# A fourth early round of expert blocks: two blocks after batch one's rows, the experts begun two steps sooner

## The chip, the cores and the metric

The kernel runs on one core of a Trainium2 chip. A core has five engines that run side by side, each in its own fixed order: TensorE (PE, matmuls; PEld is its weight load), VectorE (DVE), ScalarE (ACT), GpSimd (POOL) and SyncE (SP, which here only issues transfers). They wait for each other through semaphores. The metric is the device time of one execution in microseconds (us). The runs of the kernel before took 1124.14, 1125.73 and 1126.33 us; the median is 1125.73.

## The reference

What is computed is a two-dimensional Fourier transform per batch, of which the real part is kept, and then a mixture of eight experts of which each row uses one:

```
x: 8 batches x 2496 rows x 256
X = fft(fft(x, axis=1), axis=2).real        -> 19968 rows of 256
logits = X @ w_gate;  e = argmax(logits)    # 8 experts
gate = softmax(logits)[e];  s = sigmoid(X @ w_output_gate)[e]
out[row] = gate * s * (relu(X[row] @ w1[e]) @ w2[e])     # w1[e] 256x1024, w2[e] 1024x256
```

## The kernel before

**The transform** goes batch by batch, b = 0 to 7, and each batch has five steps (`sstage(b, i)`, i = 0 to 4), so that step n = 5b + i runs from 0 to 39. A step multiplies with tables of sines and cosines (`tst`, `tstm`, `tstr`, `tstq`; in order of i: tst, tst, tstm with tstr, tstq, tstq), DVE and ACT take the result out of PSUM (`sevac`: tiles `eo`, `rt`, `rows`), and three of the steps also do the other dimension of the next batch (`dstage`, tiles `ft` to `psb_t`, evacuated as `ahi` and `alo`). Input tiles `xt` are folded ahead of that on POOL and DVE.

**Gating and scatter.** When a batch's five steps are done, `gating(b)` chooses the expert of each row on DVE. Two small matmuls over `r_inc` count rows per expert, and from them DVE makes the row numbers `desti` in a scratch tensor `scr` in memory, in which every expert has a region of its own. POOL then scatters the batch in 20 indirect transfers (L660).

**The experts** work on blocks of 256 rows of one expert. A block needs its rows (`xr`, transposed on load, and `xf`), the expert's weights, loaded as raw tiles (`raw0b`, `raw1b`) when the expert changes and converted on ACT and DVE into two half-precision parts (`conv`: `w0b`, `w1b`), 48 matmuls of the first layer (`mm1`, tile `hp`), 48 of the second (`mm2`, tile `yp`), evacuations `hh` and `hl` between them, and an indirect transfer of the result to the output. The conversion uses scales that come from the weights' energies: before the experts, each of sixteen 1 MB weight tiles (`wt`) is loaded once and squared on ACT (`wsquare`), and `wscales` sums them by one matmul over `wen`, from which DVE makes `p_w` and the scales.

**Rounds.** Blocks are formed from the rows that are there. `BAS = (2, 4, 6)` says after how many batches a round is formed, `BLOCK = (256, 512, 512)` how many rows of an expert it takes at a time, and `NAS` follows: 12 blocks in the first round, then 6 and 10 double ones (12 and 20 blocks); a last round takes the rest when all is scattered. `table_a(k)` works out on DVE which expert and which rows each block has (`slots_a`), `slot_scales` the scales of its weights.

**Order.** SP and POOL issue in the program's order up to the first expert block and beyond; the order of PE, DVE and ACT is made by a scheduler while the kernel is built. Up to step `FSTART = 5 * BA + MARGIN0` (14) there is the transform alone. At step `WEND` (12) the tables' scales are made and the first weights are asked for. From FSTART on the experts are the foreground (`experts`) and the remaining steps the background: `rates` says how much of a step goes with each piece of a block, and `need(k)` forces steps until round k may be used. For rounds after the first, a one-element read (`fence`) of the scratch tensor orders the reads of a round behind the scatters it needs.

## Time and profile before

| what | value |
|---|---|
| median of three runs | 1125.73 us |
| the profiled execution | 1124.42 us, of which the span of instructions is 1122.7 us |
| PE busy | 1043.4 us (93%) |
| PE weight loads | 928.4 us (83%) |
| DVE busy | 819.8 us (73%) |
| ACT busy | 731.4 us (65%) |
| POOL busy | 470.8 us (42%) |
| granted PE clock, mean | 0.986 |
| steps done, by the last `tst*` matmul of a step | step 12 at 116.1, step 14 at 130.6, step 18 at 189.4, step 39 at 482.4 us |
| expert blocks done by then (of 96 matmuls) | 0, 0, 2.62, 21.50 |

The profile gives, for each engine, when it was busy and what ended its idle time. A row of the timeline shows start, duration, engine, line, operation, output<-inputs, and in brackets the idle time ahead of it with the instruction or transfer that ended it. A share of busy time over the whole span hides stages: here the first 140 us are the transform alone, then both run together until 482 us, and after that there are expert blocks only. Times in all rows count from the span's start.

### The profile page before, as it was taken

How to read it: one execution, taken by the hardware profiler on the slowest of the kernel's cores; microseconds unless marked ns; L12 is line 12 of the kernel's file. 1: busy time of each engine (PE TensorE's matmuls, PEld its weight loads, DVE VectorE, ACT ScalarE, POOL GpSimd, SP SyncE). 2: the span in 40 equal slices, each digit the busy share in tenths (PEclk: the TensorE clock that was granted, in tenths of full speed). 3: DMA queues.
4: the chain of work that ended last, by engine and by line, in shares of the span. 5: the costliest groups of instructions: out<-in, count | busy, mean ns of one | idle time of the engine just before them, and what ended most of it. 6: DMA issues, size and time to landing. Idle time of an engine off the chain costs nothing.

```text
span 1122.7 us, 28442 instructions
## 1 busy us (share of the span) xinstructions
PE 1043.4 (93%) x10020; PEld 928.4 (83%) x10020; DVE 819.8 (73%) x1526; ACT 731.4 (65%) x1214; POOL 470.8 (42%) x397
## 2 busy tenths in 40 slices
PE   5875689889899999999999999999999989999998
PEld 4664578778798899998888888899989879898887
DVE  6877797788979658587445455687777777787684
ACT  3887576667666656564454454777777777787684
POOL 0237817858577445564651221232222222322231
PEclk9997899999999999999999999999999999999999
DMA  9889476645547557668776325666657564666640
GB/s 367 314 324 334 161 189 157 172 136 175 168 142 186 141 136 185 156 168 195 202 186 165 91 66 148 185 131 170 164 159 196 142 159 127 162 186 124 184 128 30
DMA packets 158211, 194.07 MB, mean 173 GB/s; under 512 B 117885, under 2 KB 118527, under 8 KB 156020
## 3 DMA queue, kind: packets, MB, share of 16 engines
q1 hardware_dynamic: 142100, 149.68, 50.3%
q0 software_dynamic: 15824, 42.14, 11.5%
q8 instruction: 78, 1.28, 0.5%
q14 instruction: 65, 0.53, 0.1%
q10 hardware_dynamic: 144, 0.44, 0.1%
HBM read 193.47 MB, written 43.46 MB: 211 GB/s over the span
## 4 chain that ended last, share of the span: by engine, by line
PE 67%; DVE 10%; issue 8%; POOL 6%; ACT 5%; DMA 3%; SPq 1%; POOLq 0%; DVEq 0%; ACTq 0%
PE hp L1148 31%; PE yp L1168 30%; PE psb_t L524 3%; POOL scr L660 2%; POOL out_dram L1176 2%; PE psb_t L485 2%; DVE w1b L1129 2%; POOL xt L416 1%; DMA raw1b<-in_w_dram 1%; ACT w1b L1128 1%; DVE hl L1153 1%; DVE ft L431 1%; ACT wt L369 1%; DVE xt L434 1%; DVE w0b L1129 1%
## 5 line engine op out<-in xcount | busy, mean ns | idle before, releaser
L1148 PE MATMUL hp<-xr,w0b 128*128 128x256 f16 (+2 forms) x4224 | 480.0, 263 | 20.3 <-DVE hl L1153 18.6
L1168 PE MATMUL yp<-w1b,hh 128*128 128x256 f16 x2608 | 447.8, 273 | 1.7 <-ACT y L1175 1.5
L1148 PEld LDWEIGHTS <-w0b 128*128 128x128 f16 x4224 | 383.7, 98 | 69.9 <-issue 14.0
L1176 POOL DMA_INDIRECT out_dram<-y,xf x163 | 214.0, 1313 | 527.7 <-ACT y L1175 495.5
L1168 PE MATMUL yp<-w1b,hl 128*128 128x256 f16 (+3 forms) x1304 | 356.0, 273 | 0.0
L1168 PEld LDWEIGHTS <-hh 128*128 128x128 f16 x2608 | 251.1, 98 | 32.4 <-issue 3.8
L1152 ACT ACTIVATE hh<-hp 128x512 f16<-128x512 f32 (+4 forms) x352 | 194.4, 554 | 117.4 <-PE hp L1148 116.8
L1153 DVE SCALAR_TENSOR_TENSOR hl<-hp,hh 128x512 f16<-128x512 f32 (+4 forms) x352 | 221.9, 637 | 58.8 <-ACT hh L1152 58.2
L1129 DVE SCALAR_TENSOR_TENSOR w1b<-raw1b,ssc,w1b 128x1024 f16<-128x1024 f32 x144 | 189.8, 1319 | 102.2 <-ACT w1b L1128 102.0
L1129 DVE SCALAR_TENSOR_TENSOR w0b<-raw0b,ssc,w0b 128x1024 f16<-128x1024 f32 x144 | 189.3, 1318 | 60.6 <-ACT w0b L1128 60.0
L660 POOL DMA_INDIRECT scr<-rows,desti x160 | 180.5, 1128 | 66.1 <-issue 42.0
L1128 ACT ACTIVATE w0b<-raw0b,ssc 128x1024 f16<-128x1024 f32 x144 | 164.4, 1146 | 56.4 <-PE hp L1148 37.4
L1128 ACT ACTIVATE w1b<-raw1b,ssc 128x1024 f16<-128x1024 f32 x144 | 165.1, 1148 | 45.5 <-PE yp L1168 34.3
L1168 PEld LDWEIGHTS <-hl 128*128 128x128 f16 (+3 forms) x1304 | 127.6, 98 | 15.2 <-issue 0.3
L1175 ACT ACTIVATE y<-yp,ysc 128x256 f32<-128x256 f32 (+1 forms) x163 | 68.9, 470 | 47.3 <-PE yp L1168 39.9
L485 PE MATMUL psb_t<-tdet,ft 128*125 128x290 f32 (+1 forms) x200 | 57.6, 439 | 12.1 <-DVE alo L498 4.8
L416 POOL TENSOR_TENSOR xt<-xt 128x500 f32<-128x500 f32 (+1 forms) x30 | 40.5, 1357 | 51.5 <-DVE alo L498 26.4
L485 PEld LDWEIGHTS psb_t<-tdet,ft 128*125 128x125 f32 (+1 forms) x200 | 38.6, 202 | 24.8 <-issue 7.1
L524 PE MATMUL psb_t<-ahi,tstq 125*128 125x145 f16 (+1 forms) x384 | 43.1, 232 | 2.3 <-DVE alo L498 2.2
L524 PEld LDWEIGHTS <-tstq 125*128 125x128 f16 (+1 forms) x576 | 40.4, 100 | 4.4 <-issue 2.9
L431 DVE TENSOR_TENSOR ft<-xt 128x250 f32<-128x250 f32 (+1 forms) x40 | 17.4, 442 | 32.6 <-POOL xt L420 20.6
L524 PEld LDWEIGHTS <-tst 128*128 128x128 f16 (+1 forms) x384 | 27.8, 102 | 13.8 <-DVE eo L548 8.1
(214 smaller groups left out, 820.4 us busy)
## 6 DMA issues: line engine op xcount, KB each, us to landing
raw0b<-in_w_dram SPq DMA_DIRECT2D x144, 512.0 KB
raw1b<-in_w_dram SPq DMA_DIRECT2D x144, 512.0 KB
xt<-in_xl_dram SPq DMA_DIRECT2D x40, 512.0 KB
wt<-in_w_dram SPq DMA_DIRECT2D x16, 1024.0 KB
out_dram<-y,xf POOLq DMA_INDIRECT x163
scr<-rows,desti POOLq DMA_INDIRECT x160
xr<-scr SPq DMA_TRANSPOSE x88
xf<-scr SPq DMA_DIRECT2D x75, 2.0 KB
```

What stands on the lines that cost most here:

```text
L416: eng.tensor_tensor(x0, x0, x1, op=ALU.add)
L485: nc.tensor.matmul(o[:, 0:290], ft[:, k, par, W], tdab[:, k], start=(k == 0), stop=(k == 1))
L524: nc.tensor.matmul(ps[:, k, c0:c0 + 145], tab[hl][t][K], a[K, kc, par, c0:c0 + 145], start=(n == 0), stop=(n == len(terms) - 1))
L660: free_order("scr", batch=b, inst=nc.gpsimd.indirect_dma_start(out=scr[:, :], out_offset=bass.IndirectOffsetOnAxis(ap=desti[:, j:j + 1], a ...
L1128: nc.scalar.activation(w[:, 0], r, AF.Copy, scale=sc)
L1129: nc.vector.scalar_tensor_tensor(w[:, 1], r, sc, w[:, 0], op0=ALU.mult, op1=ALU.subtract)
L1148: nc.tensor.matmul(ps[:, k, T], w1v[:, hl, kc, (f % 4) * 128:(f % 4 + 1) * 128], a["x"][:, x, T], start=(m == 0), stop=(m == 5))
L1152: nc.scalar.activation(hh[:, G, T], ps[:, :, T], AF.Relu)
L1153: nc.vector.scalar_tensor_tensor(hl[:, G, T], ps[:, :, T], 0.0, hh[:, G, T], op0=ALU.max, op1=ALU.subtract)
L1168: nc.tensor.matmul(a["yp"][0:M, u], a[k, h][:, f, u * 128:u * 128 + M], w2v[:, hl, f], start=(g == 0 and f == 0 and m == 0), stop=(h == 1 ...
L1175: nc.scalar.activation(a["y"][0:M, u], a["yp"][0:M, u], AF.Copy, scale=ys[0:M, u:u + 1])
L1176: free_order("out", nc.gpsimd.indirect_dma_start(out=out[:, :], out_offset=bass.IndirectOffsetOnAxis(ap=a["f"].bitcast(I32)[0:M, u, 1:2], ...
```

## The change

There is one round more: `BAS = (1, 2, 4, 6)` and `BLOCK = (256, 256, 512, 512)`, so that two blocks are formed as soon as batch zero is scattered and ten more when batch one is; the number of blocks in all stays the same. `MARGIN0` becomes 2, so FSTART is 12 and WEND 10, and a `MARGIN1` of 4 says when the second round may be used. Round zero's table is worked out in step 5, round one's in step 10. A fence for round zero is issued on SP in step 10. The rows of blocks two and three are asked for late in block one, not two blocks ahead.

```diff
-BAS = (2, 4, 6)
-BLOCK = (256, 512, 512)
-BA = BAS[0]
+BAS = (1, 2, 4, 6)
+BLOCK = (256, 256, 512, 512)
+
+BA = 2
...
-MARGIN0 = 4
+MARGIN0 = 2
+
+MARGIN1 = 4
 FSTART = 5 * BA + MARGIN0
...
                 if i == 0 and b > 0:
+                    if n == 5 * BA:
+
+                        early(0, nc.sync.dma_start(fence, scr[DUM:DUM + 1, 0:1]))
                     add_gen(gating(b - 1))
...
-                    if b == BA:
-                        first.append(table_a(0))
-                        while next(first[0]) != "scales":
+                    if b in BAS[:2]:
+                        first.append(table_a(len(first)))
+                        while next(first[-1]) != "scales":
                             pass
...
             for n in range(NS + 1):
-                chained(load_x_, n + 2)
+                if n + 2 < NAS[0] or n >= NAS[0]:
+                    chained(load_x_, n + 2)
+                if n + 1 == NAS[0]:
+                    late_x[:] = [NAS[0], NAS[0] + 1]
...
+                    if g == 2:
+                        while late_x:
+                            chained(load_x_, late_x.pop(0))
...
-                    if k and m[1] == 5 * b + MARGIN:
+                    if k and m[1] == 5 * b + (MARGIN if k > 1 else MARGIN1):
                         ready.add(k)
...
             if m == ("step", WEND):
-                for _ in first[0]:
-                    pass
+                for f_ in first:
+                    for _ in f_:
+                        pass
...
-        work = [5 * (b - a) + (MARGIN - MARGIN0) * (i == 0) + 45 * C_TAB for i, (a, b) in enumerate(zip(BAS, BAS[1:]))] + [5 * (NB - BAS[-1]) - MARGIN + 28 * C_SCAT + 50 * C_TAB + 3.5]
-        rates = [w / (9.0 * (e - s_)) for w, s_, e in zip(work, [0] + ends, ends)]
+        work = [MARGIN1 - MARGIN0] + [5 * (b - a) + (MARGIN - MARGIN1) * (i == 0) + 45 * C_TAB for i, (a, b) in enumerate(zip(BAS[1:], BAS[2:]))] + [5 * (NB - BAS[-1]) - MARGIN + 28 * C_SCAT + 50 * C_TAB + 3.5]
+        rates = [w / (9.0 * max(e - s_, 1)) for w, s_, e in zip(work, [0] + ends, ends)]
```

How this moves instructions shows at three places. Line numbers of the changed kernel are 8 to 14 higher than before.

On PE, at the end of step 12, before: its last `tstr` matmul, then the next batch's other dimension (`psb_t<-tdet,ft`), then the matmul of the weights' energies, then step 13.

```order
L524 LDWEIGHTS tstr
L524 MATMUL psb_t<-ahi,tstr 128x145
L485 MATMUL psb_t<-tdet,ft 125x290 x8
L373 MATMUL psm_t<-wen,cs 128x16
L524 LDWEIGHTS tstq
L524 MATMUL psb_t<-ahi,tstq 128x145
```

The same place now: the first matmuls of block zero (`hp`) stand right behind step 12, with the other dimension behind them.

```order
L535 MATMUL psb_t<-alo,tstr 128x145
L535 LDWEIGHTS tstr
L535 MATMUL psb_t<-ahi,tstr 128x145
L1156 LDWEIGHTS w0b_1374
L1156 MATMUL hp<-xr,w0b_1374 128x256
```

And ahead of step 12 on PE now:

```order
L535 MATMUL psb_t<-ahi,tst_111 128x145
L496 MATMUL psb_t<-tdet,ft 125x290 x8
L384 MATMUL psm_t<-wen,cs 128x16
L611 MATMUL psm_t<-r_inc,cs 128x8
L612 MATMUL psm_t<-r_inc,cs 128x8
L474 MATMUL psm_t<-es,cs 128x1
L535 LDWEIGHTS tstm
```

The matmul over `wen` has moved from behind step 12 to ahead of it, and ahead of the two counting matmuls of batch one.

On DVE, in the gating of batch one, before (the rows that follow the first count, `r_z`):

```order
L607 TENSOR_REDUCE r_z<-r_zz 128x20
L633 TENSOR_REDUCE r_se<-r_ex 128x20
L616 TENSOR_TENSOR r_off<-psm_t,basem 128x8
L611 SCALAR_TENSOR_TENSOR r_za<-r_z 128x20
L635 TENSOR_SCALAR r_se<-r_se 128x20
L618 TENSOR_TENSOR basem<-psm_t,basem 128x8
```

The same now, up to `r_off`, from which `desti` is made:

```order
L665 COPY rows<-r_car 128x4x2 x5
L275 TENSOR_SCALAR p_w_1192<-psm_t 128x8
L275 TENSOR_SCALAR p_w_1197<-psm_t 128x8
L276 TENSOR_SCALAR p_w_1192<-p_w_1192 128x8
L277 TENSOR_SCALAR p_w_1192<-p_w_1192 128x8
L276 TENSOR_SCALAR p_w_1197<-p_w_1197 128x8
L277 TENSOR_SCALAR p_w_1197<-p_w_1197 128x8
L389 COPY wsc<-p_w_1192 128x8
L389 COPY wsc<-p_w_1197 128x8
L391 TENSOR_TENSOR wsc<-p_w_1192,p_w_1197 128x8
L627 TENSOR_TENSOR r_off<-psm_t,basem 128x8
```

The weights' scales (`p_w`, `wsc`) now stand between batch one's gating and its row numbers.

On SP, ahead of the first raw weights, before:

```order
L365 DMA wt<-in_w_dram 128x2048 x3
L304 DMA xt<-in_xl_dram 128x1024 x2
L365 DMA wt<-in_w_dram 128x2048
L304 DMA xt<-in_xl_dram 128x1024
L1090 TENSOR_LOAD slots_a_69
L1090 ISA x2
L1122 ISA
L1122 DMA raw0b_1506<-in_w_dram 128x1024
```

The same now:

```order
L376 DMA wt<-in_w_dram 128x2048 x2
L315 DMA xt<-in_xl_dram 128x1024 x2
L1005 DMA fence<-scr 1x1
L1104 TENSOR_LOAD slots_a_69
L1104 ISA x2
L1130 ISA
L1130 DMA raw0b_1370<-in_w_dram 128x1024
```

The fence stands ahead of the raw weights, and the last weight tile for the energies ahead of two input tiles instead of behind them.

More of the change, by code (lines that the diff above doesn't have):

```diff
@@ L275, in pow2_scale, with early @@
         return sc.bitcast(F32), iv.bitcast(F32)
+    def early(k, i):
+        i_ = getattr(i, "ins", i)
+        tc.add_to_no_dep_group(f"early_read{k}", i_)
+        tc.declare_no_dep(i_, group=f"late{k}", reason="rows of other batches")
+        return i
+    fence = kp.tile([1, 1], F32, name="fence")
     if True:
@@ L793, in table_a @@
             yield "scales"
-            yield from slot_scales(ea, n, i)
+            yield from slot_scales(eqall[:, o:o + n], n, i)
         def table_b():
@@ L1090, in entry @@
             return nc.sync.value_load(t[0:1, k * w + qi:k * w + qi + 1], min_val=0, max_val=hi)
-        def early(k, i):
-            i_ = getattr(i, "ins", i)
-            tc.add_to_no_dep_group(f"early_read{k}", i_)
-            tc.declare_no_dep(i_, group=f"late{k}", reason="rows of other batches")
-            return i
         def load_x_(n):
@@ L1191, in experts @@
             yield "i"
-            assert NAS[0] > 2
-            todo = []
+            assert NAS[0] >= 2
+            todo, late_x = [], []
             for n in range(NS + 1):
-                chained(load_x_, n + 2)
+                if n + 2 < NAS[0] or n >= NAS[0]:
+                    chained(load_x_, n + 2)
+                if n + 1 == NAS[0]:
+                    late_x[:] = [NAS[0], NAS[0] + 1]
                 if n == sing[0] - 4:
@@ L1226, in fft_moe_kernel @@
     ready, begun = {0}, set()
-    fence = kp.tile([1, 1], F32, name="fence")
     def background():
@@ L1235, in background @@
                 for k, b in enumerate(BAS):
-                    if k and m[1] == 5 * b + 4:
+                    if k > 1 and m[1] == 5 * b + 4:
                         for _ in table_a(k):
                             yield C_TAB
-                    if m[1] == 5 * b + MARGIN:
+                    if k and m[1] == 5 * b + (MARGIN if k > 1 else MARGIN1):
                         ready.add(k)
```

## The prediction

> **What bounds the kernel now.** I read the page's busy shares and slices first, then busy time by stretch, then the rows of single engines where TensorE (PE) has gaps.
>
> ```profile
> PE   5875689889899999999999999999999989999998
> PEclk9997899999999999999999999999999999999999
> DMA  9889476645547557668776325666657564666640
> ```
>
> A slice is 28 us. From the sixth on, PE is nearly always busy; the clock granted to it drops only in slices 4 and 5. Time can be won before about 160 us, or by closing small gaps later. The same by stretches:
>
> ```profile
> core 0: us, PE busy (x) PEld busy (x) DVE busy (x) ACT busy (x) POOL busy (x), PEclk, DMA share, GB/s
> 88.00:109.30 21.30, 7.55 (x64) 5.91 (x61) 17.06 (x72) 15.84 (x30) 16.93 (x17) 0.81 0.94 338
> 109.30:142.70 33.40, 23.08 (x189) 20.45 (x190) 26.26 (x61) 18.73 (x35) 26.36 (x23) 0.76 0.51 168
> 142.70:160.00 17.30, 14.60 (x120) 12.11 (x120) 17.30 (x47) 12.35 (x26) 2.72 (x3) 1.00 0.65 185
> 160.00:189.40 29.40, 29.40 (x289) 26.14 (x288) 22.23 (x38) 21.14 (x40) 15.67 (x13) 1.00 0.57 145
> 189.40:482.40 293.00, 276.22 (x2781) 250.54 (x2779) 224.25 (x482) 183.91 (x348) 185.07 (x162) 0.99 0.61 162
> 482.40:1122.70 640.30, 628.47 (x6076) 560.07 (x6074) 446.83 (x651) 416.31 (x617) 202.42 (x160) 1.00 0.60 151
> ```
>
> The first two rows are transform steps 12 to 15 alone, the third is the first expert block, and from 160 on PE is full. PE idles 33.40 - 23.08 = 10.3 us in the second row and 2.7 in the third; its clock of 0.76 costs another 23.08 x 0.24 = 5.5. But VectorE (DVE) idles only 4.2, 7.1, 0.0 and 7.2 us in the first four. So before 160 us DVE, not PE, is nearest to full, and only after 160 is it PE. What PE waited for:
>
> ```profile
> 100.25 0.39 PE L600 MATMUL psm_t<-r_inc,cs 128*128 128x8 f32 x2 [4.07 <-DVE r_inc L596]
> 109.29 0.30 PE L524 MATMUL psb_t<-ahi,tstm 125*128 125x145 f16 x1 [8.43 <-DVE eo L548]
> 118.05 5.84 PE L485 MATMUL psb_t<-tdet,ft 128*125 128x290 f32 x16 [1.96 <-DVE alo L498]
> 137.85 0.30 PE L524 MATMUL psb_t<-ahi,tst 125*128 125x145 f16 x1 [7.21 <-DVE eo L548]
> 142.76 2.78 PE L1148 MATMUL hp<-xr,w0b 128*128 128x256 f16 x24 [1.21 <-DMA xr<-scr]
> ```
>
> The long gaps end with DVE. The first expert matmul, at 142.76, waits for its rows, and those for the scatter of batch one on POOL:
>
> ```profile
> 72.52 1.14 POOL L660 DMA_INDIRECT scr<-rows,desti  x1 [19.66 <-DVE rows L654]
> 103.15 0.97 POOL L660 DMA_INDIRECT scr<-rows,desti  x1 [0.30 <-issue]
> 106.38 1.19 POOL L660 DMA_INDIRECT scr<-rows,desti  x1 [0.97 <-ACT r_car L646]
> 137.01 0.97 POOL L660 DMA_INDIRECT scr<-rows,desti  x1 [0.31 <-issue]
> 139.44 1.34 SPq L1108 DMA_TRANSPOSE xr<-scr  x1
> ```
>
> The first pair of rows is the first and last of twenty scatters of batch zero, the second pair of batch one, the last the issue of the first block's rows. POOL works without a break from 72.5 to 138.
>
> **The change, part by part.**
>
> *Gain: two blocks need batch zero alone*, scattered by 104. The new PE order puts 51 expert matmuls (44 of the first layer, 7 of the second) before the first `tst` matmul of step 15; before, it put none there. Not the whole two blocks (2 x 96): most of their matmuls still come after step 15. At full clock twelve take 1.31 us:
>
> ```profile
> 148.91 1.47 PE L1148 MATMUL hp<-xr,w0b 128*128 128x256 f16 x12
> 150.22 0.27 PE L1168 MATMUL yp<-w1b,hl 128*128 128x256 f16 x1
> ```
>
> (150.22 - 148.91), so 109 ns each, and 51 are **5.6 us** taken from the stretch that PE fills after 160. That the whole two blocks (21 us) fit is the upper bound; it ends at PE's idle and lost clock before 160, 10.3 + 2.7 + 5.5 = 18.5 us, and at DVE's idle, 4.2 + 7.1 + 7.2 = 18.5, less what is added to DVE (next part): 16.
>
> *Loss: one more table on DVE*, in step 5 for round zero. DVE's order has 36 instructions more than before: 29 of the kind of the first three rows here, which start 0.09 us apart, and 7 of the kind of the last two, 0.28 apart.
>
> ```profile
> 102.62 0.17 DVE L629 TENSOR_TENSOR desti<-r_dest,cs 128x20 int32<-128x20 f32 x1
> 102.71 0.17 DVE L760 TENSOR_TENSOR_SCAN r_prc<-cs,r_av 128x8 f32<-128x8 f32 x1
> 102.79 0.15 DVE L762 SCALAR_TENSOR_TENSOR r_dv<-r_av,r_dv 128x8 f32<-128x8 f32 x1
> 126.64 0.24 DVE L722 TENSOR_TENSOR r_p<-r_g,wsc 128x96 f32<-128x96 f32 x1
> 126.92 0.25 DVE L724 TENSOR_REDUCE ssc<-r_p 128x12 f32<-128x96 f32 x1
> ```
>
> 29 x 0.09 + 7 x 0.28 = 4.6 us at most. Its cover is DVE's idle time ahead of it, 21.30 - 17.06 = 4.2 us in the first stretch alone, so the least is nothing; I take **1.5**, nearer to the covered end. (4.6 is also what I take off the 18.5 above, and with DVE never quite without idle time that makes some 13 to 14 the most that can be hoped for.)
>
> *Loss: the weights' energies are finished two steps sooner.* Sixteen squares of 1 MB weight tiles on ScalarE (ACT) feed one matmul (`wen`), from which DVE takes the scales (`p_w`).
>
> ```profile
> 97.99 0.33 SPq L365 DMA_DIRECT2D wt<-in_w_dram  x1
> 106.51 1.91 ACT L369 ACTIVATE wt<-wt 128x2048 f32<-128x2048 f32 x1 [0.37 <-DMA wt<-in_w_dram]
> 103.52 0.33 SPq L365 DMA_DIRECT2D wt<-in_w_dram  x1
> 117.57 1.91 ACT L369 ACTIVATE wt<-wt 128x2048 f32<-128x2048 f32 x1
> 123.73 0.29 PE L373 MATMUL psm_t<-wen,cs 128*128 128x16 f32 x2
> ```
>
> The fifteenth load took 106.51 - 97.99 = 8.5 us to its square, since the DMA engines are full there (0.94). The sixteenth, issued at 103.52, would by that be squared from 112.0 to 113.9; before, this hurt nobody, as its matmul stood at 123.73. Now PE's order puts `wen` ahead of batch one's two `r_inc` matmuls (at 100.25 before), and DVE's order puts `p_w` ahead of the rows of the table that give batch one's destinations (102.62 before). Squares stand a little earlier in ACT's new order, so I take 112 and not 114. Then everything behind moves by 112 - 101 = 11 us: `desti` of batch one to about 114 and its first scatter from 106.4 to about 115, the last of it from 137 to about 146; the evacuation that released step 12's matmuls (109.29) to about 120, and step 12's end from 116 to about 127. DVE stands idle from its last free work at about 104.5 to 112, 7.5 us. But the old order had idle time of its own there, 33.40 - 26.26 = 7.1 us in the second stretch, and the conversions of block zero's weights (next fence) are ready to fill that. So one idle time replaces another, and I take **1.5 us** of net loss, with bounds of -3 (the last load comes early and DVE's old idle time shrinks) and +11 (all of the shift stays).
>
> *Moved: the conversions and the rows of block zero.* In SyncE's (SP's) queue a new one-element read, the fence, waits for batch zero's last scatter (103.15, and some 4 us to land) ahead of the raw weights; behind it stand those weights and then all input tiles. The raw weights went out before at 109.97, so this costs nothing; if batch zero came later, all of that would. The first weights are converted at about 120 to 126, four times 1.27 us on DVE:
>
> ```profile
> 109.97 1.52 SPq L1122 DMA_DIRECT2D raw0b<-in_w_dram  x2
> 128.42 2.66 DVE L1129 SCALAR_TENSOR_TENSOR w0b<-raw0b,ssc,w0b 128x1024 f16<-128x1024 f32 x1
> 131.50 1.27 DVE L1129 SCALAR_TENSOR_TENSOR w0b<-raw0b,ssc,w0b 128x1024 f16<-128x1024 f32 x1
> ```
>
> In SP's queue the rows of block zero stand behind two raw loads that wait for these, so they are issued at about 126.5 and used 142.76 - 139.44 = 3.3 us later, at about 130. PE is free at 127 but its next instruction is that block's first matmul, with step 13's behind it: a new gap of some 3 us. I cost it at nothing beside the 1.5 above, since DVE is at work then. Block two's rows wait for batch one as the first block's did, until about 150, with two blocks (21 us of PE) to run before; behind that wait on SP stand raw weights of blocks three and four, which have as long. Two experts more are loaded than before (round zero takes one block each of two experts, and round one comes back to them): 2 x 2 MB where the DMA engines are half idle (0.51 and 0.65), so nothing; without that idle share, as long as two tiles' 8.5 us. Steps 13 and 14 now run with two transform tiles in PSUM instead of three; PE waits for DVE there anyway, so nothing is added, and without that cover it would be one evacuation per tile.
>
> *Later.* From step 18 on the two PE orders stand level: when step 18's matmuls end, 2.62 blocks are done before and 2.67 now; at step 39, 21.50 and 21.75. Everything after that is the same work, so what is won or lost is decided before about 190 us, except for 293.00 - 276.22 = 16.8 us of small gaps up to 482, which may fall out a few us better or worse.
>
> **Sum:** -5.6 + 1.5 + 1.5 = **-2.6 us** against the profiled execution's 1124.4 us (span 1122.7), 1121.8. The median of the runs shown, 1125.7, lies 1.3 above that execution, so I predict **1123.1 us**.
>
> **Rivals.**
>
> *The gaps are filled, not shifted.* For it: PE's idle and cold 18.5 us before 160. Against: DVE, which ends nearly all of PE's gaps, has hardly more idle time than that. With half to all of the 13.5 us left after the table, -7 to -13.5, about 1115.5. Chance 0.13.
>
> *No change: the lead is eaten by the new gap and the full price of the table.* After gaps the array is slow: the sixteen matmuls of L485 took 5.84 us at 118.05, and 4.20 here:
>
> ```profile
> 91.98 4.20 PE L485 MATMUL psb_t<-tdet,ft 128*125 128x290 f32 x16 [1.25 <-DVE eo L548]
> ```
>
> If the new gap leaves the array cold, 1.6 us come on top; with them and the table at its full 4.6 the sum is -5.6 + 4.6 + 1.5 + 1.6 = +2.1, and with the table at two thirds +0.6: 1126.3 to 1127.8. For it: DVE had no idle time at all from 142.7 to 160. Against: the gap is short. Chance 0.21. The Trainium skill (TensorE: Matmul & The Clock Gate, Part 1: The HAM clock gate) says that the array falls to half its clock after an idle window of about 3.4 us and needs as long under load to come back. The granted clock of 0.76 in the stretch with the 7.2 us gap agrees; by that rule a gap of 3 us is just on the edge, and the sum would be -2.6 without and -1.0 with the 1.6.
>
> *Slower: the late matmul `wen` holds batch one back, and that stays.* For it: POOL had no break between 72.5 and 138 in which to make good a late scatter, and DVE, which waits in order, can't pass its wait for `wen`. Against: POOL is nearly idle right after, 2.72 us busy of 17.30. With all 11 us: -5.6 + 1.5 + 11 = +6.9, 1132.6. It decides as soon as more than 5.6 - 1.5 = 4.1 us of the shift are still there at step 18. Chance 0.18.
>
> *Slower: the two steps come back later.* The share of a step that goes with each block is worked out (`work`, `rates`) for eleven steps over ten blocks, and rates[0] is never used, since `ends` begins with 0; thirteen steps must be done when block ten's successor rows are asked for, so two steps are forced there in a lump. If that makes PE wait on DVE once more as at 137.85 (7.21), the sum is -2.6 + 7.2 = +4.6, 1130.3. Against: the PE orders are level again at step 25 (6.88 and 7.12 blocks). Chance 0.06.
>
> **How the numbers follow.** The forecast has 0.42, and its own range is 1119.5 to 1125 (from -6.2, when the losses are hidden, to -0.7, when one of them counts double). This kernel's runs lie within 0.2% of each other, 2.25 us, so that is what counts as a change: faster is below 1123.5, slower above 1128. Of the forecast 0.33 is faster and 0.09 no change. Faster: 0.33 + 0.13 = 0.46; no change: 0.09 + 0.21 = 0.30; slower: 0.18 + 0.06 = 0.24. The range for 8 in 10 goes from 1113, which leaves out the lowest few hundredths of the first rival, to 1131, which leaves out the upper half of the third.
>
> **What would show it.** Right: first `hp` matmul near 130 instead of 142.8; about half a block done before step 15's first matmul; step 18 done near 187 instead of 189.4 with as many blocks; `wen` between 108 and 114 with DVE idle before `p_w`, and batch one's first scatter near 115. Wrong: `wen` before 104 and no longer gap there (then the gain is larger); the stretch from step 12 to step 18 no shorter than 73 us, with PE's idle time in it as large as before (no change); step 18 after 192 (the third rival); a new PE gap of several us around steps 23 to 25 (the fourth). If the time changes by more than 5 us with step 18 in its old place, the reason lies in none of these.

## The result and the profile after

The changed kernel takes 1138.2 us (1137.07 to 1140.34), the kernel before 1125.3 beside it: a ratio of 1.0112, with an interval of 1.0094 to 1.0131. By that ratio it is **slower by about 12.6 us**; 1123.1 was forecast, and 1131 was the end of the range. One group of the runs further down, marked * in their table, took 3 to 4% longer with every kernel, the one before too (1164.3 us), so its ratios are not set against those of other groups where less than one per cent decides. The profiled execution took 1137.07 us with a span of 1135.3, 12.6 more than before. Its slices (busy tenths, 28.4 us each):

```profile
PE   6865489979889999999999999999999999999898
PEclk9898689999999999999999999999999999999999
DMA  9788747656566555667876424657667565575640
```

PE's weak stretch is the fourth and fifth slice, as before (5 and 4 tenths busy now, 5 and 6 before), but the granted clock falls to 6 and 8 in the fifth and sixth, where it was 8 and 9. By stretch, with the columns of the prediction:

```profile
core 0: us, PE busy (x) PEld busy (x) DVE busy (x) ACT busy (x) POOL busy (x), PEclk, DMA share, GB/s
88.00:109.30 21.30, 11.26 (x107) 9.19 (x105) 16.15 (x47) 18.93 (x36) 12.34 (x12) 0.90 0.91 346
109.30:123.00 13.70, 8.63 (x68) 8.38 (x68) 8.68 (x55) 6.89 (x12) 6.02 (x6) 0.53 0.70 249
123.00:147.00 24.00, 11.39 (x82) 9.00 (x82) 15.42 (x32) 11.41 (x20) 19.84 (x19) 0.72 0.79 232
147.00:170.00 23.00, 17.46 (x166) 15.41 (x167) 19.93 (x39) 12.60 (x26) 5.24 (x5) 0.85 0.38 123
170.00:203.20 33.20, 31.45 (x291) 27.07 (x289) 27.64 (x59) 22.41 (x46) 18.69 (x17) 1.00 0.69 187
203.20:498.20 295.00, 280.04 (x2800) 254.48 (x2799) 221.62 (x484) 187.16 (x350) 183.09 (x160) 0.98 0.61 162
498.20:1135.30 637.10, 627.42 (x6052) 559.04 (x6050) 444.14 (x649) 414.69 (x614) 199.11 (x158) 1.00 0.59 151
```

The stretches end where steps end: step 12 at 122.9 (116.1 before), step 13 at 147.0 (126.3), step 18 at 203.2 (189.4), step 39 at 498.2 (482.4). At step 18 there are 2.67 blocks done, and before there were 2.62: the same work, 13.8 us late. At step 39 it is 15.8 us with a quarter block more done, 2.6 us by the prediction's 109 ns a matmul, so 13.2. **All of the loss stands at 203 us**, and nearly all of it comes after 88: PE ends step 11 4.3 us late (95.1 against 90.7), but DVE starts batch one's `r_inc` only 1.4 us late (101.1 against 99.7), and w12_xf_early2, a run further down that is 3.0 us late at step 11, loses nothing. From 88 to the end of step 18, DVE was busy 82.9 of 101.4 us before (the first four rows of the prediction's table) and 87.8 of 115.2 now (the first five rows here). So of 13.8 us, 8.8 are idle time of DVE and 5.0 are more work on it. Read for PE: 26.8 us idle before, 35.0 now; and clock lost (busy time x (1 - PEclk), row by row) 7.0 before, 11.0 now.

The rows of the timeline at which this starts, of all five engines:

```profile
99.84 4.62 SPq L376 DMA_DIRECT2D wt<-in_w_dram  x2
...
109.71 1.91 ACT L380 ACTIVATE wt<-wt 128x2048 f32<-128x2048 f32 x1 [0.30 <-DMA wt<-in_w_dram]
...
111.76 0.60 PE L384 MATMUL psm_t<-wen,cs 128*128 128x16 f32 x2 [10.71 <-ACT wt L380]
...
112.41 0.24 DVE L275 TENSOR_SCALAR p_w<-psm_t 128x8 int32<-128x8 int32 x2 [5.52 <-PE psm_t L384]
...
114.81 0.17 DVE L640 TENSOR_TENSOR desti<-r_dest,cs 128x20 int32<-128x20 f32 x1
...
115.75 0.99 POOL L671 DMA_INDIRECT scr<-rows,desti  x1 [12.79 <-ACT ahi L508]
...
145.97 0.97 POOL L671 DMA_INDIRECT scr<-rows,desti  x1 [0.30 <-DMA xt<-in_xl_dram]
...
148.25 2.66 DVE L442 TENSOR_TENSOR ft<-xt 128x250 f32<-128x250 f32 x1 [4.14 <-POOL xt L427]
```

The last two weight tiles are asked for at 99.84 and squared until 111.6; PE stands 10.71 us at `wen`, DVE 5.52 at what comes out of it, and POOL 12.79 until batch one's destinations are there. POOL's twenty scatters, with the input folds (`xt`) between them, then take 31 us as before, and the folds behind them are late for DVE: the last row is one of several waits of DVE for POOL. What DVE waited for the folds from 88 us to the end of step 18, before and then now, with its other waits of 2 us and more (us in all, how often, the longest):

```profile
DVE ft L431 <- POOL xt L416: 9.4, 4, 3.1
DVE ft L431 <- POOL xt L420: 3.0, 1, 3.0
DVE alo L498 <- ACT ahi L497: 2.3, 4, 0.8
```

```profile
DVE ft L442 <- POOL xt L427: 8.9, 3, 4.1
DVE p_w L275 <- PE psm_t L384: 5.5, 1, 5.5
DVE ft L442 <- POOL xt L431: 4.1, 1, 4.1
DVE eo L559 <- ACT qb L557: 4.0, 2, 2.4
DVE rows L566 <- ACT rows L565: 2.9, 3, 1.7
```

The waits for the folds are as long as before, 13.0 us against 12.4, and the 5.5 us for `wen` came on top: the old idle time moved with the chain and was not used up. The second place where PE stands:

```profile
108.96 1.54 SPq L1130 DMA_DIRECT2D raw0b<-in_w_dram  x2
...
126.47 2.21 SPq L1130 DMA_DIRECT2D raw0b<-in_w_dram  x2
129.41 1.34 SPq L1116 DMA_TRANSPOSE xr<-scr  x1
...
135.56 2.72 PE L1156 MATMUL hp<-xr,w0b 128*128 128x256 f16 x12 [12.62 <-DMA xr<-scr]
```

PE is done with step 12 at 122.9 and waits until 135.6 for block zero's rows, with step 13 behind that wait.

### The profile page after: what moved, and what is told of

It reads as the page before. It is cut to its first block, busy times and chain, and to the rows that moved or that the text cites. A ratio compares the mean times of both kernels' runs of the same rounds, so it can differ in the third digit from the quotient of the medians.

```text
span 1135.3 us, 28467 instructions
## 1 busy us (share of the span) xinstructions
PE 1050.1 (92%) x10020; PEld 935.3 (82%) x10020; DVE 818.9 (72%) x1557; ACT 734.3 (65%) x1214; POOL 466.9 (41%) x397
## 4 chain that ended last, share of the span: by engine, by line
PE 75%; issue 6%; DVE 5%; POOL 5%; DMA 4%; ACT 3%; SPq 1%; POOLq 0%; DVEq 0%; ACTq 0%
PE hp L1156 33%; PE yp L1176 32%; PE psb_t L535 5%; PE psb_t L496 2%; POOL scr L671 2%; POOL xt L427 1%; POOL out_dram L1184 1%; DMA xt<-in_xl_dram 1%; ACT wt L380 1%; DMA xf<-scr 1%; DMA raw1b<-in_w_dram 1%; DVE ft L442 1%; ACT w1b L1136 1%; DVE w0b L1137 1%; DVE alo L509 1%
## 5 line engine op out<-in xcount | busy, mean ns | idle before, releaser
L1137 DVE SCALAR_TENSOR_TENSOR w1b<-raw1b,ssc,w1b 128x1024 f16<-128x1024 f32 x144 | 184.6, 1282 | 100.4 <-ACT w1b L1136 100.3
L1137 DVE SCALAR_TENSOR_TENSOR w0b<-raw0b,ssc,w0b 128x1024 f16<-128x1024 f32 x144 | 184.6, 1285 | 56.8 <-ACT w0b L1136 56.7
L442 DVE TENSOR_TENSOR ft<-xt 128x250 f32<-128x250 f32 (+1 forms) x40 | 19.7, 498 | 36.6 <-POOL xt L431 22.2
L535 PE MATMUL psb_t<-alo,tstq 125*128 125x145 f16 (+1 forms) x192 | 39.3, 231 | 0.0
```

Of the source, the lines that this page charges most:

```text
L535: nc.tensor.matmul(ps[:, k, c0:c0 + 145], tab[hl][t][K], a[K, kc, par, c0:c0 + 145], start=(n == 0), stop=(n == len(terms) - 1))
L1137: nc.vector.scalar_tensor_tensor(w[:, 1], r, sc, w[:, 0], op0=ALU.mult, op1=ALU.subtract)
```

## The experiments

Each group of runs was timed beside the kernel before on the same chip, and the ratio is to that; * marks the longer group named above. "Level" is the end of step 18, less 10.45 us (96 x 109 ns) for each block done beyond 2.62: what the kernel would show there with the work of the kernel before. It comes from one profiled execution and follows the timed differences to some 3 us (w10_start13, the worst, is 3.7 off).

| run | us | ratio [interval] | wen | scatters of batch one | first hp | level |
|---|---|---|---|---|---|---|
| before | 1125.7 | 1 | 123.7 | 106.4 to 137.0 | 142.8 | 189.4 |
| the change | 1138.2 | 1.0112 [1.0094, 1.0131] | 111.8 | 115.8 to 146.0 | 135.6 | 202.7 |
| b_wen10 | 1135.2 | 1.0079 [1.0053, 1.0106] | 113.1 | 117.1 to 148.0 | 153.8 | 198.8 |
| wend12 | 1128.9 | 1.0024 [1.0009, 1.0038] | 120.0 | 108.4 to 139.0 | 141.3 | 193.9 |
| r4_start14 | 1131.0 | 1.0040 [1.0023, 1.0056] | 121.8 | 108.5 to 137.9 | 143.8 | 195.2 |
| w10_start13 | 1135.3 | 1.0078 [1.0050, 1.0106] | 113.4 | 117.4 to 147.7 | 144.5 | 201.9 |
| b_sq10 | 1127.3 | 1.0009 [0.9993, 1.0025] | 115.4 | 107.9 to 139.3 | 145.1 | 191.6 |
| wend12_xfirst | 1126.7 | 1.0006 [0.9989, 1.0024] | 118.4 | 106.8 to 137.4 | 130.8 | 190.9 |
| a_noenergy | 1125.5 | 0.9992 [0.9973, 1.0011] | - | 100.7 to 132.6 | 124.6 | 190.9 |
| b_noenergy | 1119.6 | 0.9933 [0.9909, 0.9957] | - | 106.9 to 136.1 | 142.6 | 184.8 |
| after_xfirst* | 1178.4 | 1.0102 [1.0073, 1.0132] | 113.4 | 117.4 to 148.4 | 125.0 | 207.1 |
| start13_xfirst* | 1172.2 | 1.0064 [1.0039, 1.0089] | 115.8 | 108.0 to 138.7 | 134.4 | 200.2 |
| r4_start14_xfirst* | 1172.3 | 1.0072 [1.0049, 1.0096] | 121.5 | 109.3 to 139.2 | 134.6 | 197.4 |
| a_noen_xfirst* | 1170.6 | 1.0042 [1.0018, 1.0066] | - | 102.9 to 135.5 | 125.9 | 194.7 |
| b_table2 | 1125.1 | 0.9997 [0.9983, 1.0011] | 120.9 | 108.0 to 137.5 | 144.0 | 190.0 |
| a_noen_wend12 | 1124.5 | 0.9981 [0.9961, 1.0001] | - | 102.7 to 133.5 | 132.0 | 187.9 |
| a_noen_w12_x | 1119.4 | 0.9949 [0.9934, 0.9965] | - | 99.0 to 130.8 | 117.4 | 184.2 |
| b_noen_again | 1120.5 | 0.9954 [0.9942, 0.9965] | - | 105.8 to 135.5 | 141.2 | 183.9 |
| wend12_xf_again | 1127.7 | 1.0014 [1.0001, 1.0028] | 119.1 | 107.5 to 138.2 | 131.5 | 192.2 |
| w12_xf_early2 | 1124.1 | 0.9979 [0.9962, 0.9995] | 119.8 | 108.2 to 138.9 | 132.2 | 189.6 |

### The early energies alone, and taken back

b_wen10 is the kernel before with the energies finished two steps sooner, and nothing else of the change:

```diff
-                while wk <= 2 * E and wk < (n + 1) * (2 * E + 1) / WEND:
+                while wk <= 2 * E and wk < (n + 1) * (2 * E + 1) / (WEND - 2):
```

> The kernel before (three rounds, experts from step 14) with one edit: the sixteen weight squares and the matmul over wen are finished by the end of step 9 instead of step 11, so that wen stands ahead of batch one's counting matmuls on TensorE, as in the changed kernel. Theory A (the loss is the early wen, which waits for the last weight tile and holds batch one's row numbers, scatters and folds back): batch one's first scatter near 115 instead of 106.4, the last near 146 instead of 137, and 1133 to 1138 us. Theory B (the loss is block zero's matmuls standing on TensorE ahead of step 13, where they wait for rows): no such matmuls here, so within 3 us of before, 1123 to 1128. Theory C (the fourth round's table and order alone): also within 3 us of before.

wend12 is the change with the energies at their old step (and the tables' scales with them), so that `wen` stands behind batch one's `r_inc` again. It moves block zero's first matmuls as well: they come within step 14 on PE instead of ahead of step 13, with 0.25 of a block done by the end of step 14, where the change has 0.53:

```diff
-WEND, NW = FSTART - 2, 2
+WEND, NW = FSTART, 2
```

> The changed kernel (four rounds, experts from step 12) with one edit: WEND is FSTART and not FSTART - 2, so the weights' energies are finished by step 11 as in the kernel before, and wen stands behind step 12. Theory A: the loss is gone, 1121 to 1128 us, batch one's first scatter near 106. Theory B: block zero's first matmuls now stand behind step 13 but still ahead of step 14 and wait for rows that come later still (first weights converted near 127, rows near 134), so a gap of 5 us or more ahead of them stays and half or more of the 13 us: 1131 to 1138. Theory C: no change against the changed kernel, 1135 to 1140.

w10_start13 keeps the energies early (`MARGIN0 = 3`, `WEND = FSTART - 3`) and begins the experts a step later, which also leaves 0.25 of a block by the end of step 14:

> The changed kernel with the early energies (wen by the end of step 9, ahead of batch one's counting matmuls) but the experts from step 13, so that on TensorE block zero's first matmuls stand behind step 13 and not ahead of it. Theory A: the loss stays, 1133 to 1139 us, batch one's first scatter near 115. Theory B: most of the loss is gone, 1124 to 1130, since TensorE no longer waits 12.6 us for block zero's rows with step 13 behind them. If both count, 1129 to 1134.

The energies alone make the kernel before slower by 0.79%, and taken back they make the change faster by 0.88%, 9.9 us; wend12's 1128.9 is 1 us over theory A's range. The later start without them taken back leaves 0.78%. So of the 0.88%, 0.54% (6.1 us, w10_start13 less wend12) are the energies with block zero within step 14 in both, and 0.34% are the later place of block zero; that part is not shown, since the intervals of the change and of w10_start13 overlap. The rows of b_wen10 show the chain of the changed kernel:

```profile
113.11 0.61 PE L373 MATMUL psm_t<-wen,cs 128*128 128x16 f32 x2 [13.71 <-ACT wt L369]
...
116.15 0.17 DVE L629 TENSOR_TENSOR desti<-r_dest,cs 128x20 int32<-128x20 f32 x1
...
117.10 0.99 POOL L660 DMA_INDIRECT scr<-rows,desti  x1 [10.22 <-ACT ahi L497]
...
148.03 0.97 POOL L660 DMA_INDIRECT scr<-rows,desti  x1 [0.30 <-issue]
```

Is it the place of `wen` in the order, or the loads and squares, which come sooner too? b_sq10 spreads the squares as b_wen10 does and leaves the matmul at its old step:

```diff
-                while wk <= 2 * E and wk < (n + 1) * (2 * E + 1) / WEND:
+                while wk <= 2 * E and wk < (n + 1) * (2 * E + 1) / (WEND - 2 if wk < 2 * E else WEND):
```

> The kernel before, with the sixteen squares of the weights and their loads spread over ten steps as in the change, but the matmul `wen` and the scales left in step 11, behind batch one's `r_inc` matmuls. Theory A (what costs is the place of the matmul `wen` in TensorE's order, ahead of batch one's `r_inc`, because batch one's destinations then wait for the last weight load): batch one's first scatter comes at 106 to 110 as before, step 18 ends at 188 to 192, and the time is that of before, 1123 to 1129 us. Rival theory L (what costs are the loads and squares themselves, which crowd ScalarE and the DMA queues in steps 5 to 9, wherever the matmul stands): step 18 ends near 198 as in the run with both, and the time is 1132 to 1137 us. In between, 1129 to 1132, both have a share.

It is as fast as the kernel before. Its rows:

```profile
115.36 0.34 PE L373 MATMUL psm_t<-wen,cs 128*128 128x16 f32 x2
...
107.93 1.55 POOL L660 DMA_INDIRECT scr<-rows,desti  x1 [2.86 <-issue]
...
139.28 0.98 POOL L660 DMA_INDIRECT scr<-rows,desti  x1 [0.30 <-issue]
```

The sixteenth square began at 112.1 here, 111.05 in b_wen10: the same. But PE reaches `wen` after batch one's `r_inc`, waits for nothing, and batch one is scattered at the old time. So **one matmul's place costs 0.70% in the kernel before (b_wen10 less b_sq10, 7.9 us)**; in the change, finishing the energies early costs 0.54% (w10_start13 less wend12). That is about half to two thirds of the loss of 1.12%.

### The fourth round alone

r4_start14 is the change with the old start (`MARGIN0 = 4`) and round one taken as ready from the start (`ready = {0, 1}`): only the round of two blocks is left.

> The changed kernel with the experts from step 14 and the energies by step 11, both as before (MARGIN0 4), so that of the change only the fourth round is left: one more table on VectorE in step 5, two blocks after batch zero, ten after batch one. Theory A: within 4 us of before, 1121 to 1129, and if anything a little faster since block zero need not wait for batch one's scatter (its rows before 139). Theory B: the same, since no expert matmul stands ahead of step 15. Theory C: 1134 to 1140, like the changed kernel.

It is slower by 0.40%, which no theory expected: A and B had it level or faster, C as slow as the change. Its rows of the timeline show where:

```profile
136.75 1.46 SPq L1116 DMA_TRANSPOSE xr<-scr  x1
...
143.82 2.72 PE L1156 MATMUL hp<-xr,w0b 128*128 128x256 f16 x12 [14.60 <-ACT rows L565]
```

PE's order has block zero's first matmuls ahead of step 15, and they wait 14.6 us: batch zero has been scattered since 102, but SP asks for the rows at 136.75, behind raw loads that wait for the first weights to be converted. (The row names ACT's `rows`; it ended at 143.7, and the transfer of the rows landed within 0.1 us of that.) In the runs named xfirst, SP asks for blocks zero's and one's rows right after the four raw loads of block zero:

```diff
                     chained(load_w, 0, m, h)
+            chained(load_x_, 0)
+            chained(load_x_, 1)
             for h in range(2):
                 conv(0, 0, h)
             yield "w"
-            chained(load_x_, 0)
             hold.clear()
-            chained(load_x_, 1)
```

> The change with the energies at their old place (as in the run `wend12`, 1128.9 us), and besides, SyncE issues block zero's rows right behind the four raw loads of block zero's first weights, ahead of the raw loads that wait for conversions. Theory X (what is left of the loss is that block zero's rows are issued at 132 behind those waits, so that its matmuls stand and wait at the head of TensorE's queue): rows issued at 110 to 118, first `hp` before 133, step 18 at 187 to 191 instead of 194.5, and 1121 to 1126 us. Rival theory T (what is left is work: the table of round zero, its DMAs and two experts more, and the first weights' conversions are late anyway): first `hp` still waits for its weights until 138 or later, step 18 stays at 193 to 196, and the time is 1127 to 1131 us.

> The change whole, with the early `wen`, and block zero's rows issued ahead of the raw loads that wait for conversions. With the late `wen` the same edit took the time from 1128.9 to 1126.7 us, 2.3 us. If the two losses are separate and add up (theory S), the time is 1138.2 - 2.3 = 1136, from 1134 to 1137 us, with batch one's first scatter still at 113 to 117 and the first `hp` before 133 instead of 135.6. If the wait for the rows was most of what the early `wen` costs in the change (rival theory W), 1128 to 1133 us.

> The change with the experts' start one step later (MARGIN0 = 3, so that `wen` stands behind batch one's `r_inc` and block zero's first matmuls behind step 14's first ones), and block zero's rows issued early. Theory X (with `wen` behind `r_inc` and the rows early, the matmuls of block zero find their operands and the lead is kept): no gap over 3 us before the first `hp`, step 18 at 186 to 191, 1121 to 1125 us. Rival theory D (VectorE is full there, so that a lead in one place is paid in another): step 18 at 192 to 196, 1125.5 to 1130 us.

> The fourth round alone at the old start of the experts (as in the run `r4_start14`, 1131.0 us, where the first `hp` stood 14.6 us waiting for rows issued at 136.7), with block zero's rows issued early. Theory X: that gap shrinks to 0 to 4 us, the first `hp` comes at 129 to 135, and the time falls by 5 to 9 us, to 1122 to 1126. Rival theory D: the rows come early and VectorE or the weights' conversions then end the same gap; 1127 to 1131 us.

With the late `wen` the rows are asked for at 118 and the first `hp` runs at 130.8; the time is that of the kernel before, 1.0006 and, when it was run again, 1.0014, against 1.0024 without the edit. These intervals overlap, so a gain of the edit, 1 to 2 us, is likely and not shown. The time of 1126.7 lies between the ranges of theories X and T. With the early `wen` it changes nothing that can be seen (1.0102 against 1.0112, of two groups that are not to be compared so finely; theory W's 1128 to 1133 us is out within its own group, theory S's small gain is not): PE's gap ahead of `hp` shrinks from 12.6 to 2.8 us, and a gap of 8.2 opens behind it, ended by DVE's `rt`, which reads step 12's tile in PSUM. start13_xfirst and r4_start14_xfirst show the same: `hp` waits for at most 1.2 us, and gaps of 6.9 and 7.8 ended by DVE stand at 150.7 and 146.4. In these two, theory X was right on the rows and wrong on the time: both are slower than the kernel before of their own group, by more than theory D's ranges too.

### Without the energies

In the next runs the loads and squares of the weights are left out, and the sums of squares are a constant, so that these kernels leave the true scales out and the time is that of all the rest. a_noenergy is the change so, b_noenergy and b_noen_again the kernel before; a_noen_xfirst has the rows early, a_noen_wend12 has block zero's matmuls behind step 14's first (`WEND = FSTART`), a_noen_w12_x both.

> The change without the energies of the weights: their loads, squares and reads of them are left out and the sums of squares are a constant, so that the scales are wrong and the time is that of the rest. Beside the same edit of the kernel before. Theory A (the early `wen` is most of the loss, and nothing else of the change holds batch one back): batch one's first scatter comes at 100 to 108, and the change is within 5 us of the kernel before with the same edit, or faster by up to the 5.6 us that were forecast. Rival theory T (the fourth round costs by itself, with DVE full and its rows late): the change is still 3 to 8 us slower than the kernel before with the same edit.

> The kernel before without the energies of the weights: loads, squares and reads left out, the sums of squares a constant, so that the scales are wrong and the time is that of the rest. Sixteen loads of 1 MB where the DMA engines are full (share 0.94 from 88 to 109) and 31 us of ScalarE go: step 12 ends at 108 to 115 instead of 116, step 18 at 180 to 188 instead of 189.4, and 1115 to 1124 us. It is the measure for the run of the change with the same edit; both theories expect the same of it.

> The change without the energies of the weights (left out as in the run `a_noenergy`, so that the scales are wrong), and block zero's rows issued early. The change without the energies took 1125.5 us, the kernel before without them 1119.6; its first `hp` stood 13.8 us. Theory X (the 5.9 us between the two are this wait for the rows): the gap shrinks to under 4 us and the time is 1117 to 1121. Rival theory T (they are the work of the fourth round, its table and its two experts more): 1123 to 1126 us.

> The change without the energies of the weights (left out, scales wrong, as in `a_noenergy`), with block zero's first matmuls behind step 14's first one in TensorE's order, where `a_noenergy` had twelve of them ahead of step 13 and TensorE stood 13.8 us at them. Theory P (that place in the order is what costs): the gap before the first `hp` is under 4 us and the time is 4 to 8 us below `a_noenergy`, by ratios to the kernel before 0.992 to 0.996. Rival theory T (the fourth round's work on VectorE costs, wherever the matmuls stand): within 2 us of `a_noenergy`, ratio 0.997 to 1.001.

> As `a_noen_wend12` and block zero's rows issued early as well: everything that the runs have shown to hold the fourth round back is out of the way, the energies too. If the forecast gain of two early blocks exists at all (theory P), this is 2 to 8 us faster than the kernel before with the same energies left out (`b_noen_again`), whose ratio was 0.9933: 0.986 to 0.9915. Theory T: no faster than it, ratio 0.993 to 0.998.

> The kernel before without the energies once more (scales wrong), as the measure for the two others on the same chip: ratio to the kernel before 0.991 to 0.996, as it was 0.9933.

With no energies to wait for, the change is still slower than the kernel before without them, by 0.6% (0.9992 against 0.9933), as theory T had it. The rows early leave the gap at `hp` as it was, 13.5 us after 13.8, so the place of SP's issue alone does not explain it, and theory X was wrong on the gap; the time of a_noen_xfirst has no partner without the energies in its group. SP asked for the rows at 110.5 there, and it was DVE that ended the gap:

```profile
124.91 0.76 DVE L554 SCALAR_TENSOR_TENSOR rt<-psb_t,qb 128x258 f32<-128x258 f32 x2
...
125.93 2.72 PE L1157 MATMUL hp<-xr,w0b 128*128 128x256 f16 x12 [13.52 <-DVE rt L554]
```

`hp` reads nothing of `rt`; that it waited for the place in PSUM which `rt` empties is likely and not shown. With the matmuls one step later alone (0.9981) little is won; with both (0.9949) the change is level with the kernel before (0.9954), and no faster. So even there the fourth round brought **nothing that can be seen**. The stretch behind 131 us, of b_noen_again and then of a_noen_w12_x, up to the end of step 18 in each:

```profile
131.00:183.90 52.90, 46.34 (x411) 39.34 (x409) 44.14 (x91) 34.52 (x69) 25.85 (x22) 0.94 0.57 158
```

```profile
131.00:190.50 59.50, 53.80 (x493) 45.65 (x490) 46.83 (x95) 37.06 (x73) 27.73 (x25) 0.94 0.72 193
...
160.00 0.39 PE L612 MATMUL psm_t<-r_inc,cs 128*128 128x8 f32 x2 [2.74 <-DVE r_inc L608]
...
162.48 5.30 PE L1157 MATMUL hp<-xr,w0b 128*128 128x256 f16 x24 [1.86 <-DMA xr<-scr]
```

a_noen_w12_x has 0.60 blocks more done at step 18, 6.3 us of matmuls, and comes there 6.6 us later. PE idles 5.7 us in this stretch and 6.6 in the other, but not at the same place. In b_noen_again the 6.6 are two gaps, 4.8 ahead of the first `hp` and 1.8 ahead of a transform step, and this stretch of a_noen_w12_x has neither. In a_noen_w12_x 4.6 of the 5.7 us are the gaps of the last two rows: PE waits for DVE's count, then block two for its rows, which SP asks for at 156.9 only, and the 24 matmuls behind take 5.30 us, where the first 24 of the kernel before took 2.78. So the early matmuls did fill gaps, but new gaps and slow matmuls, 7.1 us in all (4.6 + 2.5), stand at the hand-over to the second round. This run was meant to have every hindrance out of the way, and it had not.

### The second table alone

b_table2 is the kernel before with round zero's table made twice, the first time in step 5 as in the change (30 instructions more on DVE); `slot_scales` reads `eqall` as in the change.

```diff
-                    if b == BA:
+                    if b in (1, BA):
                         first.append(table_a(0))
-                        while next(first[0]) != "scales":
+                        while next(first[-1]) != "scales":
```

> The kernel before with round zero's table made twice: first in step 5 (30 instructions more on VectorE, about as many as the change adds), then as before in step 10. Nothing else moves by intent. Theory T (the table is dear: VectorE has little idle time there and the instructions that wait behind it delay batch zero's scatter or the transform): 4 to 8 us slower than the kernel before on the same chip, ratio 1.0035 to 1.007. Theory Q (its 4.6 us lie in VectorE's idle time, nearly all): at most 2 us slower, ratio 0.999 to 1.002. The prediction's term was +1.5 us, within 0 to 4.6.

0.9997 [0.9983, 1.0011]: theory Q. Step 8 ends later in the trace (84.6 us, 78.1 before) and step 12 at 117.1 (116.1): what the table takes, the idle time ahead of step 12 gives back.

### Block two's rows sooner

In w12_xf_early2 SP asks for block two's rows during block zero, four raw loads sooner than in wend12_xfirst; the scheduler's order of PE around them shifts a little with it.

```diff
-                if n + 1 == NAS[0]:
-                    late_x[:] = [NAS[0], NAS[0] + 1]
+                if n < 2:
+                    late_x.append(NAS[0] + n)
```

> As `wend12_xfirst` (late `wen`, block zero's rows early; 1126.7 us, ratio 1.0006), with block two's rows issued four raw loads sooner on SyncE, during block zero instead of block one. Theory H (what is left of the loss is the hand-over to the second round: TensorE waits 3.2 us in two gaps at 167 to 171 and then runs at a lower clock, because those rows are issued at 165): rows of block two issued before 158, no gap at their use, step 18 two to four us sooner for the same blocks, and the time 2 to 4 us under the base: ratio 0.997 to 0.9985. Rival theory D (VectorE sets that stretch, and rows that are there sooner wait for it): ratio 0.9995 to 1.002, as its base.

> `wend12_xfirst` once more, as the base on the same chip: ratio to the kernel before 0.999 to 1.0025 (it was 1.0006), with two gaps of 1 to 2 us around 167 to 171 and block two's rows issued at about 165.

The first rows are of wend12_xf_again, the next of w12_xf_early2:

```profile
165.00:196.00 31.00, 26.74 (x244) 22.64 (x242) 23.63 (x53) 18.95 (x37) 16.71 (x16) 0.94 0.85 213
...
165.69 1.28 SPq L1116 DMA_TRANSPOSE xr<-scr  x1
...
176.34 2.60 PE L1156 MATMUL hp<-xr,w0b 128*128 128x256 f16 x12 [1.32 <-DVE hl L1161]
```

```profile
165.00:196.00 31.00, 28.25 (x276) 24.49 (x273) 23.62 (x50) 18.95 (x37) 14.20 (x11) 1.00 0.82 192
...
147.53 1.28 SPq L1116 DMA_TRANSPOSE xr<-scr  x1
...
169.30 1.48 PE L1156 MATMUL hp<-xr,w0b 128*128 128x256 f16 x12 [1.26 <-DVE hl L1161]
```

Asked for at 147.5 instead of 165.7, PE is busy 1.5 us more and at full clock: 1.5 + 26.74 x 0.06 = 3.1 us, and the time is 3.6 us (0.3%) under its base. Two gaps of 1.3 and 1.5 us stay. Theory H's time held, though it expected no gap there. This is **the one version that beat the kernel before**, by 0.21% [0.05, 0.38]; its twelve runs spread from 1119.3 to 1127.1 us, so the size is uncertain. How much of it is the rows and how much the changed order of PE, these runs don't tell apart.

## Why the prediction was wrong, step by step

**The chain behind `wen` was right to the microsecond.** Forecast: `wen` at 112, `desti` at about 114, the first scatter at 115, the last at 146. Measured: 111.8, 114.8, 115.8, 146.0. Step 12's end was put at 127 and came at 122.9.

**Its price is the step that failed.** The shift of 11 us was counted as 1.5 net, because "one idle time replaces another", between -3 and +11. It cost 6 to 8 us (w10_start13 against wend12, b_wen10 against b_sq10). The old idle time of DVE was not replaced: in the stretch from 109.3 to 123 DVE idled 5.0 us, from 123 to 147 another 8.6 and up to 170 3.1, where it had 7.1 and 0.0 before. The reason that the prediction itself gave for the rival holds: POOL had no break in which to make good a late scatter, and what came out late behind the scatters, the folds, is what DVE then waited for, as long as before (13.0 us against 12.4), with the 5.5 us for `wen` on top. So the third rival was the right one, and it was given 0.18. Its condition ("more than 4.1 us of the shift still there at step 18") was met by far; its time of 1132.6 was 5.6 us too low, as much as the gain that it still counted. That the rest of its sum, 11 for the shift and 1.5 for the table, comes to the 12.6 measured is luck: the shift cost 6 to 8 and the table nothing that can be seen, and block zero's place and late rows, priced at nothing, make up the difference.

**The new gap ahead of block zero was costed at nothing, "since DVE is at work then".** It was 12.6 us, not 3, since PE was free at 122.9 and not 127, and the rows came at 135.6 and not 130: SP issued them at 129.4 (126.5 was forecast), and they took 6.2 us, not the 3.3 of the row that was read. DVE was busy 15.4 of 24 us there, so the cover was not whole. Where the gap was mostly taken away and `wen` stayed (after_xfirst), the time did not follow; where block zero came a step later (w10_start13), the loss was smaller by 0.34%, not clear of the noise. The fence, in the same part, did cost nothing: the raw weights left at 108.96, and at 109.97 before.

**The gain of 5.6 us did not come.** 51 matmuls did come ahead of step 15 (0.53 of a block by step 14, as forecast 0.5), but matmuls that come sooner gain only what they put into gaps that do not open again. Without the energies and with block zero's rows early (a_noen_w12_x against b_noen_again) the ratios are 0.9949 and 0.9954, each known to some 0.15%: at best 0.3%, and by the medians 1 us. There the gaps opened again at block two's rows, of which the prediction said that they have two blocks (21 us of PE) of cover; asked for sooner, they gave the 0.21% of w12_xf_early2, 2.4 us. No run leaves out the energies and has block two's rows sooner, so how much of the 5.6 is to be had stays open. The prediction had said that DVE, not PE, is nearest to full before 160 us, and then counted the gain on PE. Which of DVE's instructions set the pace in that stretch was not worked out further.

**The table** was taken at 1.5 us between 0 and 4.6; it costs 0 within 1.5 (b_table2). Its covered end was right. (In the forecast's own range the terms give -5.6 with both losses hidden and -1.1 with one counted double, where it says -6.2 and -0.7; nothing hangs on it.)

**What is not settled:** the change with the late `wen` is 0.24% slower than before. The order of PE and of SP around block zero's and block two's rows carries it (0.9979 where both are moved), but the share of each lies within the intervals. Two more terms that the prediction put at nothing have no run of their own: two transform tiles in PSUM instead of three in steps 13 and 14, and the weights of two experts more. r4_start14, which keeps three tiles up to step 14, is 0.40% slower all the same, so the tiles are not the whole of it.

**The other rivals.** Gaps filled: no. No change: no; the cold array that spoke for it is there, though (next section). The two steps that come back in a lump: one gap of 4.8 us stands in step 22 (at 248.5, ended by DVE's `hl`), but PE's gaps from step 18 to 39 sum to 15.0 us, 16.8 before, so no. Among the signs that the prediction named, "step 18 after 192 (the third rival)" decided, with 203.2.

## What to carry to other kernels

An instruction that waits for a transfer takes everything behind it on its engine with it: before something is finished sooner, look which chain it is put ahead of, and whether that chain's last engine has a break in which to make good. Here the same early squares were free with the small matmul behind `r_inc`, and cost 8 us ahead of it. A shift is only paid by idle time if that idle time belongs to the same chain: count the engine that comes last in it (here POOL's 31 us of scatters and folds), not the sum of idle time on an engine in the middle. And work taken ahead gains only if what follows it is ready sooner too: here two early blocks filled PE's old gaps, and new ones opened where the third block waited for its rows.

## What the hardware showed that was not expected

**A block's rows took about twice as long to load beside other transfers.** From issue to the first matmul that waited for them: 3.3 us before (139.44 to 142.76, when the scatters were over), 6.2 in the change (129.41 to 135.56) and 7.1 in r4_start14 (136.75 to 143.82), with scatters (in r4_start14 the last two) and weight loads in flight. The scatters are not needed for it: in a_noen_w12_x block two's rows took 5.6 us (156.91 to 162.48), with batch one's last scatter at 130.8, batch two's not begun, and raw weights asked for at 149.78 and 155.82. What each adds was not tried.

**Two short gaps together made the array slow.** In a_noen_w12_x PE idled 2.74 and 1.86 us with 0.61 us of `r_inc` matmuls of eight columns between them; the granted clock from 162.4 to 166 was 0.50, and the 24 matmuls behind the gaps took 5.30 us, where 24 such took 2.78 at full clock. The Trainium skill (TensorE: Matmul & The Clock Gate, Part 1: The HAM clock gate) gives an idle window of about 3.4 us, which runs free, as what slows the array, and as long under load to bring it back. Neither gap is that long; together with the small matmuls they are 5.2 us, so the trace agrees with the rule only if so little work counts as idle. In the change itself the 10.71 us ahead of `wen` were followed by a granted clock of 0.53 up to 123, as the rule has it. The matmuls that began at 116.2 came to full pace at 121.9, after 5.7 us, which a window of that length that runs free allows.
